# Scaling the tokens on ScalarE inside a mixture-of-experts unit, and adding the first product ahead of VectorE's other sums

## The chip, the cores and the metric

The kernel runs on one core of one Trainium2 chip. Its time is measured in microseconds on the device, as the median of several executions. One execution was also recorded by the hardware profiler; all rows below come from that one.

## The reference, cut to what matters

Attention with a sliding window gives 4608 tokens of 512 numbers. They go through eight experts, and every token's expert outputs are added with the weights of a Sinkhorn routing:

```python
for e in range(E):                       # E = 8
    h = np.maximum(x @ w1[e], 0.0)       # x: 4608 x 512, w1[e]: 512 x 1024
    ye = h @ w2[e]                       # w2[e]: 1024 x 512
    out += P[:, e:e + 1] * ye            # P: routing weights, 4608 x 8, none negative
```

Because no weight is negative, x may be multiplied by its weight before the first product: relu(P x w1) w2 = P relu(x w1) w2.

## The kernel before

The kernel has two parts. The first computes attention, gates and the Sinkhorn iterations, and with them experts 0 and 1 of all tokens, whose outputs it keeps in DRAM (`ysp`). The second part is the loop over `units` (N = 108). A unit is one expert `e` from 2 to 7 for one group `g` of 256 tokens (two blocks `m` of 128); the six experts of a group follow each other, and there are 18 groups. The order of all instructions is written out by hand: each engine executes its own in the order in which the code issues them, and waits only for data and for buffers.

A unit has two layers. The first layer of unit n is computed in step n of the loop, the second layer of unit n - 1 in the same step, woven between the first one's matmuls, so that TensorE always has something to do.

- **The first layer.** For experts 2 to 6, from step 6 on (85 units), it is a Strassen product with seven partial products (`part`, L968). They use three PSUM banks `pa`, `pb`, `pc` out of a pool of four (`pmm`), which are handed out in turn. ScalarE copies sums from bank to bank (L1114, L1118, L1123) and applies the relu (`relu`, L981); VectorE makes the slots 3 and 1 of `h` from PSUM and `s5` (L1128, L1132). The other units use four plain banks (`l1_bank`, L948, its relu on L957).
- **The second layer** (`product`, L1005) is seven Strassen products too, numbered 1 to 7. Each goes on summing into its half of a PSUM bank `psM` over the six experts of a group. Product 1 has a bank of its own, and is the last one issued in a step. `make_sums` (VectorE, L985 to L987) makes its operands from `h`.
- **The end of a group.** When the last expert of a group is through (`end`), `gather` (VectorE, L1047) adds products 3, 4, 5 and 2 out of PSUM into `acc` in the step after; in the step after that (`done`), it adds 6, 7 and 1, and `finish` stores `acc`. Matmuls of the next group have then begun to refill these banks: the product m of the new group's first expert overwrites the bank, and so waits for the `gather` of the old product m.
- **The tokens.** `load_x` brings a group's two blocks into `xtok`. `scale_x(n + 2)` multiplies them by the routing weights of the unit after next (L889; 128x512, half precision, the weight of a token being one number for each partition) into `xs`; `turn_xs(n + 2)` has two DMAs transpose them into `xset` (L901, issued by SP), and `sums_x` (VectorE, L913 to L915) makes the sums T1 to T4 that the Strassen parts read. When `scale_x` has scaled for expert 7, it loads the next group's tokens (L881).
- **The start of a group's sum.** `begin` (VectorE, L1020, L1023) sets `acc` to the weighted outputs of experts 0 and 1, one block in each of two steps. In the first group `xtok` lies in the memory of `acc`, so `begin` must come after the last `scale_x` of that group.

Before the loop, `scale_x(0)` and `scale_x(1)` are issued among the last matmuls of the first part (the "filler", whose relu is L127 and whose matmuls are L115 and L137).

VectorE's order in a step before the change: `make_sums`, in a `done` step products 6 and 7 into `acc`, `scale_x`, `begin` where due, L1128, L1132, in a `done` step product 1 into `acc`, `sums_x`.

Of the kernel before, what the change touches and what calls it, by code (L numbers as in the profile page):

```python
# [14 lines left out]
def kernel(  # L15
# [10 lines left out]
    nc = tc.nc  # L26
    AF = mybir.ActivationFunctionType
    ALU = mybir.AluOpType
# [50 lines left out]
    P_sb = L_sb  # L79
# [149 lines left out]
    if True:  # L229
# [459 lines left out]
        for n, (b, kb, u) in enumerate(steps):  # L689
# [94 lines left out]
            if 10 * b + at >= 66:  # L784
                i = 10 * b + at - 66
# [39 lines left out]
        for it in range(8):  # L825
# [4 lines left out]
                out=P_sb,  # L830
                in0=P_sb,
# [4 lines left out]
                out=cs_sb, in_=P_sb.rearrange("p c e -> p e c"), axis=AX.X, op=ALU.add  # L836
# [8 lines left out]
                out=P_sb,  # L845
                in0=P_sb,
                scalar=float(Ntok) / float(E),
                in1=ca_sb.unsqueeze(1).to_broadcast([P, NBLK, E]),
                op0=ALU.mult,
# [13 lines left out]
        units = [(g, e) for g in groups for e in range(2, E)]  # L863
# [9 lines left out]
        xtok = [acc.rearrange("p m d -> p (m d)").bitcast(FP16)[:, HD * i : HD * i + HD] for i in range(2)]  # L873
        xs = [xset[i // 2][:, 4 + 2 * (i % 2) : 6 + 2 * (i % 2), :].rearrange("p q n -> p (q n)") for i in range(4)]
# [4 lines left out]
        def load_x(g):  # L879
            for m in range(2):  # L880
                nc.sync.dma_start(out=xtok[m], in_=xd[2 * g + m])  # L881

        def scale_x(n):
            if n >= N:
                return
            g, e = units[n]
            for m in range(2):
                blk = 2 * g + m
                nc.vector.tensor_scalar(  # L889
                    out=xs[2 * (n % 2) + m], in0=xtok[m], scalar1=P_sb[:, blk, e : e + 1], scalar2=None, op0=ALU.mult  # L890
                )
            if e == E - 1 and n + 1 < N:
                if g == groups[0]:
                    xtok[:] = [per.tile([P, HD], FP16, name=f"xtok_{i}", tag="yo", bufs=YO) for i in range(2)]
                load_x(units[n + 1][0])
# [43 lines left out]
        def l1_bank(n, i):  # L939
            g, e = units[n]  # L940
            if i == 0:
                new_h(n)
            x = xset[n % 2][:, 0:4].rearrange("p q (d t) -> p (q d) t", t=P).rearrange("p (b d) t -> p d b t", b=2)
            ps = aps.tile([P, 2, HB], FP32, name=f"psh_{n}_{i}", tag="pmm", bufs=4)
            for f in range(2):
                ft = 2 * i + f
                for dt in range(NDT):
                    nc.tensor.matmul(  # L948
                        out=ps[:, f, :],
                        lhsT=W1L[e][:, dt, P * ft : P * ft + P],  # L950
                        rhs=x[:, dt],
                        start=(f == 0 and dt == 0),
                        stop=(dt == NDT - 1),
                        skip_group_check=True,
                    )
            fh, j = 2 * (i // 2), 2 * (i % 2)
            nc.scalar.activation(  # L957
                out=h[n][:, fh : fh + 2, j : j + 2, :].rearrange("p t f k -> p f t k"),
                in_=ps.rearrange("p f (t k) -> p f t k", t=2),
                func=AF.Relu,  # L960
            )
# [18 lines left out]
        def relu(n, slot, src):  # L980
            nc.scalar.activation(out=h[n][:, slot], in_=src, func=AF.Relu)  # L981
# [14 lines left out]
        def product(n, *which):  # L996
            if n < 0:
                return
            g, e = units[n]
            for m in which:  # L1000
                bk, half = BANK[m]
                if bk not in Ms:
                    Ms[bk] = mps.tile([P, 2, 2 * P], FP32, name=f"psM_{bk}")
                for f in range(NF2):
                    nc.tensor.matmul(  # L1005
                        out=Ms[bk][:, half, :],
                        lhsT=h[n][:, LEFT[m], f, :],
                        rhs=W2L[e][RIGHT[m]][:, f, :],
                        start=(e == 2 and f == 0 and half == 0),
                        stop=(ends(n) and f == NF2 - 1 and (half == 1 or m == 1)),  # L1010
                        skip_group_check=True,
                    )
# [5 lines left out]
        def begin(g, m):  # L1018
            blk = 2 * g + m
            nc.vector.tensor_scalar(  # L1020
                out=acc[:, m, :], in0=y[:, 0, m, :], scalar1=P_sb[:, blk, 0:1], scalar2=None, op0=ALU.mult
            )
            nc.vector.scalar_tensor_tensor(  # L1023
                out=acc[:, m, :], in0=y[:, 1, m, :], scalar=P_sb[:, blk, 1:2], in1=acc[:, m, :],
                op0=ALU.mult, op1=ALU.add,
            )

        def gather(g, *which):
            q4 = acc.rearrange("p m (c n) -> p (m c) n", c=2)
            for m in which:  # L1030
                bk, half = BANK[m]
                ps = Ms[bk][:, half, :]
                for lo, step, op in {
                    1: ((0, 3, ALU.add),),
                    2: ((2, 0, ALU.add), (3, 0, ALU.subtract)),
                    3: ((1, 2, ALU.add),),
                    4: ((0, 2, ALU.subtract),),
                    5: ((0, 0, ALU.subtract), (1, 0, ALU.add)),
                    6: ((3, 0, ALU.add),),
                    7: ((0, 0, ALU.subtract),),  # L1040
                }[m]:
                    if step:
                        a = q4[:, lo : lo + step + 1 : step, :]
                        p2 = ps.unsqueeze(1).to_broadcast([P, 2, HB])
                    else:
                        a, p2 = q4[:, lo, :], ps
                    nc.vector.tensor_tensor(out=a, in0=a, in1=p2, op=op)  # L1047
# [46 lines left out]
        for n in range(N):  # L1094
            g = units[n - 1][0]
            end = ends(n - 1)
            done, late = late, ()
            if n > 0:
                make_sums(n - 1)
            some((4, 1, 0, 3, 2)[n] if n < 5 else 0)  # L1100
            if 0 < n <= E - 3:
                quads_w1(units[n - 1][1])
            if done:
                gather(units[n - 2][0], 6, 7)
            scale_x(n + 2)
            if n > 0 and units[n - 1][1] in (4, 5):
                begin(g, units[n - 1][1] - 4)
            if strassen(n):
                new_h(n)
                s5 = s5s[:, n % 2]  # L1110
                pa = bank(n, "A")
                part(n, pa, "a11", B11, True)
                pb = bank(n, "B")
                nc.scalar.copy(out=pb, in_=pa)  # L1114
                product(n - 1, 3)
                pc = bank(n, "C")
                part(n, pc, "s1", T1, True)
                nc.scalar.copy(out=s5, in_=pc)  # L1118
                product(n - 1, 4)
                if end:  # L1120
                    gather(g, 3, 4)
                part(n, pb, "s2", T2)
                nc.scalar.copy(out=pc, in_=pb)  # L1123
                part(n, pa, "a12", B21)
                relu(n, 0, pa)
                product(n - 1, 5, 2)
                part(n, pb, "s3", T3)
                nc.vector.tensor_tensor(out=h[n][:, 3], in0=pb, in1=s5, op=ALU.add)  # L1128
                relu(n, 3, h[n][:, 3])
                part(n, pc, "s4", B22)  # L1130
                turn_xs(n + 2)
                nc.vector.tensor_tensor(out=h[n][:, 1], in0=pc, in1=s5, op=ALU.add)  # L1132
                relu(n, 1, h[n][:, 1])
                if done:
                    gather(units[n - 2][0], 1)
                sums_x(n + 1)
                if end:
                    gather(g, 5, 2)
                product(n - 1, 6, 7)
                part(n, pb, "a22", T4)  # L1140
                relu(n, 2, pb)
                product(n - 1, 1)
            else:
                if done:
                    gather(units[n - 2][0], 1)
                pairs = ((3, 4), (5, 2), (6, 7), (1,))
                for i in range(4):
                    l1_bank(n, i)
                    product(n - 1, *pairs[i])
                    if end and i in (0, 1):  # L1150
                        gather(g, *pairs[i])
                turn_xs(n + 2)
                sums_x(n + 1)
            if done:
                finish(units[n - 2][0])
            if n > 0 and units[n - 1][1] == 2:
                load_y(g)
            if end:
                late = (6, 7, 1)
            if n == N - E + 2:  # L1160
                load_w2(E - 1)
# [34 lines left out]
```

## Time and profile before

| | |
|---|---|
| three runs | 1035.68, 1036.04 and 1041.56 us; median 1036.04 |
| the profiled execution | 1037.82 us, of which the span of the records is 1034.8 us |
| TensorE matmuls busy | 1008.6 us, 97% of the span |
| VectorE busy | 765.8 us, 74% |
| ScalarE busy | 566.8 us, 55% |
| the scaling, L889 on VectorE | 216 instructions of 347 ns (204 of them from `xtok`: 62.1 us) |
| TensorE clock granted | 0.998 |

In the rows, PE is TensorE's matmuls, PEld its weight loads, DVE VectorE, ACT ScalarE, POOL GpSimd, SP the engine that issues most DMAs. A row of the timeline gives the start, the length, the engine, the line and operation, what is written and read, and in brackets how long the engine stood idle before and what ended that. A row of the waits gives who waited for whom: the sum, how often, and the longest. A row of the groups gives, after the bar, the busy time in us and the mean ns of one instruction.

### The profile page before, as it was taken

How to read it: one execution, taken by the hardware profiler on the slowest of the kernel's cores; microseconds unless marked ns; L12 is line 12 of the kernel's file. 1: busy time of each engine (PE TensorE's matmuls, PEld its weight loads, DVE VectorE, ACT ScalarE, POOL GpSimd, SP SyncE). 2: the span in 40 equal slices, each digit the busy share in tenths (PEclk: the TensorE clock that was granted, in tenths of full speed). 3: DMA queues.
4: the chain of work that ended last, by engine and by line, in shares of the span. 5: the costliest groups of instructions: out<-in, count | busy, mean ns of one | idle time of the engine just before them, and what ended most of it. 6: DMA issues, size and time to landing. Idle time of an engine off the chain costs nothing.

```text
span 1034.8 us, 26710 instructions
## 1 busy us (share of the span) xinstructions
PE 1008.6 (97%) x11079; PEld 803.6 (78%) x11079; DVE 765.8 (74%) x1720; ACT 566.8 (55%) x973; POOL 80.4 (8%) x143
## 2 busy tenths in 40 slices
PE   7999999999999999999999999999999999999998
PEld 5645444444544789999999999999999999999997
DVE  5735666656587698778777877877877877877876
ACT  6646554555333345555555555655655655655654
POOL 1313032315110000000000000000000000000000
PEclk9999999999999999999999999999999999999999
DMA  9997799889997323324423423424433432432461
GB/s 245 203 259 174 152 224 232 204 187 186 226 186 146 88 56 93 83 52 93 84 52 93 95 45 89 103 43 87 99 57 78 94 71 64 98 76 59 97 119 37
DMA packets 264427, 122.38 MB, mean 118 GB/s; under 512 B 201969, under 2 KB 255729, under 8 KB 264305
## 3 DMA queue, kind: packets, MB, share of 16 engines
q1 hardware_dynamic: 249568, 102.68, 43.4%
q0 software_dynamic: 14304, 17.84, 10.4%
q8 instruction: 86, 1.41, 0.6%
q14 instruction: 37, 0.29, 0.1%
q10 hardware_dynamic: 432, 0.16, 0.1%
HBM read 78.30 MB, written 23.59 MB: 98 GB/s over the span
## 4 chain that ended last, share of the span: by engine, by line
PE 66%; DVE 14%; issue 2%; DMA 0%; SPq 0%; ACT 0%; DVEq 0%
PE psM L1005 25%; PE psB L968 8%; PE psy L137 7%; PE psh L115 7%; PE psh L948 7%; PE psA L968 6%; PE psC L968 5%; DVE acc L1047 4%; DVE hs L1132 2%; DVE hs L986 1%; DVE hs L985 1%; DVE hs L1128 1%; DVE hs L987 1%; PE psN L468 1%; DVE xset L913 1%
## 5 line engine op out<-in xcount | busy, mean ns | idle before, releaser
L1005 PEld LDWEIGHTS <-hs 128*128 128x128 f16 x2996 | 275.8, 98 | 35.0 <-issue 10.0
L1005 PE MATMUL psM<-w2l,hs 128*128 128x256 f16 x1440 | 186.6, 273 | 0.4 <-DVE hs L985 0.4
L968 PEld LDWEIGHTS <-w1l 128*128 128x128 f16 x2720 | 173.3, 98 | 4.0
L981 ACT ACTIVATE hs<-hs 128x512 f16<-128x512 f16 x170 | 104.3, 630 | 124.5 <-DVE hs L1128 124.5
L115 PE MATMUL psh<-xT,w1t 128*128 128x512 f16 (+1 forms) x608 | 139.7, 368 | 2.8 <-DVE xT L517 2.4
L127 ACT ACTIVATE hT<-psh 128x512 f16<-128x512 f32 (+1 forms) x144 | 83.5, 586 | 103.8 <-PE psh L115 103.3
L1005 PE MATMUL psM<-more,hs 128*128 128x256 f16 x864 | 128.9, 272 | 8.0 <-DVE acc L1047 8.0
L137 PE MATMUL psy<-w2t,hT 128*128 128x512 f16 x576 | 134.3, 379 | 0.0
L985 DVE TENSOR_TENSOR hs<-hs 128x1024 f16<-128x1024 f16 x107 | 73.8, 690 | 80.4 <-ACT hs L957 53.6
L968 PEld LDWEIGHTS <-s 128*128 128x128 f16 x1632 | 108.3, 98 | 4.6
L957 ACT ACTIVATE hs<-psh 128x512 f16<-128x512 f32 x92 | 55.0, 597 | 98.9 <-PE psh L948 96.6
L968 PE MATMUL psA<-xset,w1l 128*128 128x128 f16 x1360 | 103.7, 219 | 0.0
L137 PEld LDWEIGHTS <-hT 128*128 128x128 f16 x576 | 53.5, 98 | 60.9 <-issue 1.5
L555 DVE CAST yo<-psy 128x512 f16<-128x512 f32 x68 | 46.9, 690 | 69.8 <-PE psy L137 61.8
L115 PEld LDWEIGHTS <-w1t 128*128 128x128 f16 x608 | 54.7, 98 | 54.2 <-issue 6.3
L1128 DVE TENSOR_TENSOR hs<-psB,s5s 128x512 f16<-128x512 f32 x85 | 58.7, 690 | 41.8 <-PE psB L968 41.7
L430 ACT ACTIVATE pt<-psS 128x1024 f16<-128x1024 f32 (+2 forms) x80 | 67.7, 851 | 31.7 <-PE psS L412 24.5
L968 PE MATMUL psB<-xset,s 128*128 128x128 f16 x1088 | 82.9, 219 | 0.0
L1047 DVE TENSOR_TENSOR acc<-acc,psM 128x256 f32<-128x256 f32 (+1 forms) x162 | 73.9, 502 | 1.1 <-PE psM L1005 1.1
L948 PE MATMUL psh<-xset,w1t 128*128 128x256 f16 x576 | 74.6, 273 | 0.0
L443 DVE TENSOR_TENSOR pt<-pt,mask 128x1024 f16<-128x1024 f16 (+2 forms) x80 | 50.4, 630 | 32.0 <-ACT pt L430 31.9
L986 DVE TENSOR_TENSOR hs<-hs 128x1024 f16<-128x1024 f16 x107 | 73.2, 684 | 0.0
(113 smaller groups left out, 1386.6 us busy)
## 6 DMA issues: line engine op xcount, KB each, us to landing
y<-ysp SPq DMA_DIRECT2D x36, 256.0 KB, 3.2
ysp<-yo SPq DMA_DIRECT2D x68, 128.0 KB, 3.1
v<-in_v_dram SPq DMA_DIRECT2D x32, 256.0 KB, 4.6
out_dram<-acc SPq DMA_DIRECT2D x31, 256.0 KB, 2.6
q<-in_q_dram SPq DMA_DIRECT2D x5, 1024.0 KB, 6.6
k<-in_k_dram SPq DMA_DIRECT2D x5, 1024.0 KB, 9.2
xtok<-xd SPq DMA_DIRECT2D x34, 128.0 KB, 2.1
w2t<-in_moe_w_dram POOLq DMA_DIRECT2D x4, 1024.0 KB, 10.5
```

The source lines that it names most:

```text
L115: nc.tensor.matmul(out=ps[:, 0:nt], lhsT=w1ts[e][:, dt, P * ft : P * ft + P], rhs=xT[:, at : at + nb, dt, :], start=(dt == 0), stop=(dt == ...
L127: nc.scalar.activation(out=st["hT"][:, ft, 0:nt], in_=ps[:, 0:nt], func=AF.Relu)
L137: nc.tensor.matmul(out=ps, lhsT=st["hT"][:, ft, P * ms : P * ms + P], rhs=w2ts[e][:, ft, :], start=(ft == 0), stop=(ft == NFT - 1),)
L430: nc.scalar.activation(out=pt[0:nk, :, 0 : nk + nn], in_=ps[0:nk, :, :, 0 : nk + nn].rearrange("p a y n -> p (a y) n"), func=AF.Exp, scale ...
L948: nc.tensor.matmul(out=ps[:, f, :], lhsT=W1L[e][:, dt, P * ft : P * ft + P], rhs=x[:, dt], start=(f == 0 and dt == 0), stop=(dt == NDT - 1 ...
L968: nc.tensor.matmul(out=ps[:, j, :], lhsT=SL[e][w][:, k, P * j : P * j + P], rhs=xset[n % 2][:, x, P * k : P * k + P], start=(start and j = ...
L981: nc.scalar.activation(out=h[n][:, slot], in_=src, func=AF.Relu)
L985: nc.vector.tensor_tensor(out=t[:, 4:6], in0=t[:, 0:2], in1=t[:, 2:4], op=ALU.add)
L986: nc.vector.tensor_tensor(out=t[:, 6:8], in0=t[:, 1:4:2], in1=t[:, 0:3:2], op=ALU.subtract)
L1005: nc.tensor.matmul(out=Ms[bk][:, half, :], lhsT=h[n][:, LEFT[m], f, :], rhs=W2L[e][RIGHT[m]][:, f, :], start=(e == 2 and f == 0 and half = ...
L1047: nc.vector.tensor_tensor(out=a, in0=a, in1=p2, op=op)
L1128: nc.vector.tensor_tensor(out=h[n][:, 3], in0=pb, in1=s5, op=ALU.add)
```

## The change

`scale_x` multiplies on ScalarE (`nc.scalar.mul`) instead of VectorE. Its call moves from the head of the step into it: in a Strassen step behind the relu of `pa`, in a plain step behind the second bank. The `gather` of product 1 moves from behind the sums out of PSUM (L1128, L1132) to directly behind that of products 6 and 7. `begin` comes one step later.

```diff
-                nc.vector.tensor_scalar(
-                    out=xs[2 * (n % 2) + m], in0=xtok[m], scalar1=P_sb[:, blk, e : e + 1], scalar2=None, op0=ALU.mult
-                )
+                nc.scalar.mul(out=xs[2 * (n % 2) + m], in_=xtok[m], mul=P_sb[:, blk, e : e + 1])
...
             if done:
                 gather(units[n - 2][0], 6, 7)
-            scale_x(n + 2)
-            if n > 0 and units[n - 1][1] in (4, 5):
-                begin(g, units[n - 1][1] - 4)
+                gather(units[n - 2][0], 1)
+            if n > 0 and units[n - 1][1] in (5, 6):
+                begin(g, units[n - 1][1] - 5)
             if strassen(n):
...
                 part(n, pa, "a12", B21)
                 relu(n, 0, pa)
+                scale_x(n + 2)
                 product(n - 1, 5, 2)
...
                 relu(n, 1, h[n][:, 1])
-                if done:
-                    gather(units[n - 2][0], 1)
                 sums_x(n + 1)
...
             else:
-                if done:
-                    gather(units[n - 2][0], 1)
                 pairs = ((3, 4), (5, 2), (6, 7), (1,))
                 for i in range(4):
                     l1_bank(n, i)
+                    if i == 1:
+                        scale_x(n + 2)
                     product(n - 1, *pairs[i])
```

## The prediction

> **What bounds the kernel now.** I read the page first, then the waits of TensorE, then the timeline of two units of the last stage.
>
> ```profile
> span 1034.8 us, 26710 instructions
> ...
> PE 66%; DVE 14%; issue 2%; DMA 0%; SPq 0%; ACT 0%; DVEq 0%
> ```
>
> ```profile
> PE psM L1005 <- DVE acc L1047: 8.0, 17, 0.6
> ...
> PE psM L1005 <- DVE hs L985: 0.4, 1, 0.4
> ```
>
> The chain that ended last is mostly TensorE, with 14% on VectorE. The waits say where VectorE gets into it: TensorE stood 17 times, 8.0 us in all, before a product into PSUM (L1005) until VectorE had added an older product into `acc` (L1047). There are 18 groups, and 17 of them are followed by another one, so this is one stall for each change of group. Ordinary units have none. An ordinary Strassen unit, from its first matmul (`psA`, 703.95) to that of the next (710.13) and that one's third bank (`psC`):
>
> ```profile
> 703.95 0.61 PE L968 MATMUL psA<-xset,w1l 128*128 128x128 f16 x8
> ...
> 706.42 0.57 ACT L1123 COPY psC<-psB 128x512 f32<-128x512 f32 x1 [0.35 <-PE psB L968]
> ...
> 706.90 0.60 ACT L981 ACTIVATE hs<-psA 128x512 f16<-128x512 f32 x1
> ...
> 708.20 0.69 DVE L1128 TENSOR_TENSOR hs<-psB,s5s 128x512 f16<-128x512 f32 x1 [0.25 <-PE psB L968]
> ...
> 708.92 1.23 ACT L981 ACTIVATE hs<-hs 128x512 f16<-128x512 f16 x2 [1.42 <-DVE hs L1128]
> ...
> 710.06 0.58 ACT L981 ACTIVATE hs<-psB 128x512 f16<-128x512 f32 x1
> ...
> 710.13 0.61 PE L968 MATMUL psA<-xset,w1l 128*128 128x128 f16 x8
> ...
> 711.01 0.61 PE L968 MATMUL psC<-xset,aux 128*128 128x128 f16 x8
> ```
>
> It takes 710.13 - 703.95 = 6.18 us. ScalarE idles 1.42 us in it, between the first relu (706.90) and the two that wait for VectorE's sums (708.92). Now the second unit of a group, the one in which `done` is set:
>
> ```profile
> 614.81 0.61 PE L968 MATMUL psA<-xset,w1l 128*128 128x128 f16 x8
> ...
> 617.76 0.60 ACT L981 ACTIVATE hs<-psA 128x512 f16<-128x512 f32 x1
> ...
> 618.72 0.61 DVE L889 TENSOR_SCALAR xs<-xtok,L_sb 128x512 f16<-128x512 f16 x2
> ...
> 619.24 0.68 DVE L1128 TENSOR_TENSOR hs<-psB,s5s 128x512 f16<-128x512 f32 x1
> ...
> 619.96 1.23 ACT L981 ACTIVATE hs<-hs 128x512 f16<-128x512 f16 x2 [1.60 <-DVE hs L1128]
> 620.11 0.61 PE L968 MATMUL psB<-xset,w1l 128*128 128x128 f16 x8
> 620.44 0.68 DVE L1047 TENSOR_TENSOR acc<-acc,psM 128x512 f32<-128x512 f32 x1
> ...
> 621.10 0.58 ACT L981 ACTIVATE hs<-psB 128x512 f16<-128x512 f32 x1
> 621.17 0.60 PE L1005 MATMUL psM<-more,hs 128*128 128x256 f16 x4 [0.45 <-DVE acc L1047]
> ...
> 621.61 0.61 PE L968 MATMUL psA<-xset,w1l 128*128 128x128 f16 x8
> ...
> 622.49 0.61 PE L968 MATMUL psC<-xset,s 128*128 128x128 f16 x8
> ```
>
> It takes 621.61 - 614.81 = 6.80 us, 0.62 more than an ordinary one. The product at 621.17 starts a new sum in the bank of product 1, and that bank is free only when the add of the old product 1 (620.44 to 621.12) has read it. That add stands last of VectorE's queue here, behind the two scalings (618.72) and the two sums out of PSUM (619.24 and the one after it). Nothing forces it there: the old product 1 was finished before this unit began.
>
> **The change, part by part.** (1) *The add of product 1 goes in front.* In the `done` unit it takes the place of the two scalings, which leave VectorE. It then runs at about 618.7 to 619.4, over 1 us ahead of 620.56, when TensorE could use the bank (620.11 plus the 0.45 that eight such matmuls take from start to start). The stall's full price is not the 0.45 shown, because a matmul's shown end comes later than the start of the next one: it is 621.17 - 620.56 = 0.61, which the 0.62 of the two unit lengths confirms. Over all 17: 8.0 us shown plus 17 x 0.16 for that overlap = 10.7 us. The stalls vary little, the longest being 0.6 as shown.
>
> What is late next: the sum out of `psB` (L1128). It stood behind two scalings and now stands behind one add:
>
> ```profile
> L981 ACT ACTIVATE hs<-hs 128x512 f16<-128x512 f16 x170 | 104.3, 630 | 124.5 <-DVE hs L1128 124.5
> ...
> L889 DVE TENSOR_SCALAR xs<-xtok,L_sb 128x512 f16<-128x512 f16 x204 | 62.1, 347 | 0.0
> ...
> L1047 DVE TENSOR_TENSOR acc<-acc,psM 128x512 f32<-128x512 f32 x54 | 35.2, 679 | 0.6 <-PE psM L1005 0.6
> ...
> L235 ACT ACTIVATE mask<-rel 128x256 f16<-128x256 f16 x8 | 2.8, 404 | 0.0
> ...
> L823 ACT ACTIVATE L_sb<-L_sb,mx_sb 128x288 f32<-128x288 f32 x1 | 0.5, 534 | 0.0
> ```
>
> The pair held VectorE 0.52 from start to the next start (618.72 to 619.24), the add about 0.60 (0.68 less the 0.08 by which neighbours overlap), so L1128 and the three relus behind it come 0.08 later: the last relu at 621.18, ending 621.76. The next unit's third bank is the one that this relu reads (four banks in turn, three for a unit). Its first matmul moves from 622.49 to 622.49 - 0.61 = 621.88. Slack 0.12, less some 0.04 for a semaphore. I take 0; bounds 0 and 17 x 0.3 = 5 us given back.
>
> (2) *The scaling on ScalarE*: 216 instructions, two for each of 108 units. The trace has no such instruction (half-precision source, a column of `P_sb` as the scale). Rows around it: the relu from SBUF, same size, 630 ns; the only activation with a per-partition operand (L823, 128x288) 534 ns, which scaled by 512/288 is at most 949; from below the 0.57 of the copy at 706.42. Between L235 and L823 lie 130 ns for 32 more columns and the operand, about 100 for the operand alone, so I take 630 + 100 = 730 ns, an estimate, and 0.64 from start to start, since activations that wait for nothing overlap 0.09 (706.42 + 0.57 against 706.90).
>
> In the ordinary unit the pair starts at about 707.41 and ends at 708.78; the next relu is released at 708.92. Nothing is later. Room there: 1.51 us until that relu slips, and 0.37 more until TensorE sees it, through the third bank of the next unit (the last relu ends 710.64, its bank is written at 711.01): 1.88 for the pair, 0.94 each. The 949 as a duration is 0.86 from start to start, so TensorE is not reached even at the upper bound. In the `done` unit the pair starts at 618.27, relu 3 is due at 620.04, slack 0.4.
>
> From the Trainium skill, "ScalarE: Activation LUTs", section "What ACT_TABLE_LOAD costs": an activation takes 186 ns + 0.833 per column and 93 for each per-partition operand. By that a scaling is 706 ns, an estimate from the page; the relu of the trace, 630, stands beside its 613; no run here has shown the operand yet, and the sum would be the same.
>
> In the units without Strassen (the last of each group and the first six) the pair goes between the relus of the second and the third bank:
>
> ```profile
> 606.64 0.60 ACT L957 ACTIVATE hs<-psh 128x512 f16<-128x512 f32 x1 [1.15 <-PE psh L948]
> ```
>
> A gap of 1.15 for a pair of 1.28: that relu comes some 0.1 late, the next gap takes it up; 0.
>
> (3) *What waits for the scaling.* It moves about 1.9 us back in the unit, and SP's queue with it: the loads of `xtok` (one unit of six) and the transposes stand behind it.
>
> ```profile
> 706.53 0.82 SPq L881 DMA_DIRECT2D xtok<-xd  x2
> ```
>
> ```profile
> L901 SPq DMA_TRANSPOSE xset<-xs x212: 1188/1192/2542, 345.4 to 1013.4; - x106
> ...
> DMA to landing us min/median/max: 2.4/2.5/5.7
> ```
>
> ```profile
> L881 SPq DMA_DIRECT2D xtok<-xd x34: 332/375/925, 362.1 to 973.5; - x34
> ...
> DMA to landing us min/median/max: 2.0/2.1/4.3
> ```
>
> Worst unit, with both: loads 708.8 to 709.6, transposes issued at 709.6 and 710.8, landed 713.3; their reader is the unit after next, from 703.95 + 2 x 6.18 = 716.3. The new `xtok` lands at 709.2 + 2.1 = 711.3 and is read by the next unit's pair at 713.6. If it were late, ScalarE's queue would hold three relus behind it. Price 0, with 2 to 3 us to spare.
>
> (4) *`begin` one unit later* (1.2 us of VectorE): it falls into units where VectorE idles before L1128 or has no Strassen sums: 0. In the first group it clears a wait:
>
> ```profile
> 374.60 1.04 PE L948 MATMUL psh<-xset,w1t 128*128 128x256 f16 x8
> ...
> 375.99 1.05 PE L1005 MATMUL psM<-w2l,hs 128*128 128x256 f16 x8 [0.35 <-DVE hs L985]
> ```
>
> Eight such matmuls go on after 0.87, here after 1.39: 0.5 us, a gain that I take; bounds 0 and 0.5.
>
> (5) *The four scalings ahead of the loop* now stand between relus of the last filler unit and wait for their loads:
>
> ```profile
> 325.36 0.90 SPq L881 DMA_DIRECT2D acc<-xd  x2
> ...
> 328.69 0.60 ACT L127 ACTIVATE hT<-psh 128x512 f16<-128x512 f32 x1 [1.99 <-PE psh L115]
> ...
> 331.08 3.62 PE L115 MATMUL psh<-xT,w1t 128*128 128x512 f16 x16
> ```
>
> ```profile
> acc<-xd SPq DMA_DIRECT2D x2, 128.0 KB, 3.2
> ```
>
> Loads land at 328.6 and 329.0, the four end at about 331.2, and the relu of 328.69 ends at 331.8 instead of 329.3. Its bank is wanted again by the second half of the run at 331.08, at 331.95. I take 0; up to 0.9 if a load lands 1.1 later, as one `xtok` did (4.3 beside the 3.2 here).
>
> **Sum.** 10.7 + 0.5 = 11.2 us off. The profiled execution took 1037.82 us (span 1034.8 and 3.0 around it), so 1026.6 by it. The median of the three runs is 1036.04, 1.8 below; on that basis 1024.8, or 1.08% less. One per cent, 10.4 us, is about what a measurement of this kernel can tell from no change, so the gain lies just beyond it.
>
> **The rivals.** *The wait is handed on.* With the add gone from the end, the third bank of the next unit is 0.08 away from being next. For it: that thin slack, on a chain (add, L1128, three relus) each link of which may be some hundredths longer. Against: ordinary units run the same chain without a wait. Given back 0.3 of each 0.62: 17 x 0.3 = 5.1, so 1030; all given back, about 1035.5.
>
> *ScalarE becomes the bound: slower.* Place: the relus behind the pair in all 85 Strassen units. Point: more than 0.94 us for each scaling from start to start. If one costs twice the relu from SBUF (1.26, or 1.17 start to start), each unit loses 2.34 - 1.88 = 0.46: 39 us against the 11 won, so 1064. Against: L823 shows no such factor. A rule speaks for it: the Trainium skill, "ScalarE: Activation LUTs", section "Rules for kernel authors", wants plain multiplications on VectorE, not ScalarE. The trace agrees on the single instruction (347 against 630 and more), but an instruction in ScalarE's 1.42 of idle time displaces nothing.
>
> *The change doesn't do what it says*: the stall has another cause, and the add's place is chance. Then 1036. Against it: the add ends at 621.12 and the product starts at 621.17.
>
> **How the numbers follow.** Forecast, all or nearly all of the stalls gone: 0.72 (1023.5 to 1027.5). Handed on in part, or another cause: 0.19 (1028 to 1036). Slower: 0.09. Predicted 1024.8. The range runs from 1022.5 (the same stalls a little dearer than shown) to 1031, the middle of the second case; about 0.15 lies outside. Faster by over 1% needs more than 10.4 of the 11.2, that is all of the small terms going as taken: 0.60. Within 1%: the rest of the forecast and most of the second case, 0.31. Slower by over 1%: 0.09.
>
> **What would show it.** Right: no wait of `psM` for `acc` among TensorE's waits; the `done` unit at 6.2 us; scalings of 0.65 to 0.75 us on ScalarE, and its wait for L1128 down from 1.42 to about 0.15; transposes about 1 us later with no wait of `psh` or of L913 for them. Wrong: a wait of `psC` for the relu of `psB`, or of `psA`, in the unit after a `done` unit; relus that start straight after a scaling in every unit; ScalarE waiting for `xtok`; or a `done` unit still at 6.8.

## The result, and the profile after

The changed kernel takes 1027.84 us (median of five runs, 1025.04 to 1028.74) against 1037.38 for the kernel before (1035.68 to 1041.56). The ratio of the means is 0.9898, with a 95% interval from 0.987 to 0.9927; that of the medians is 0.9908. So the change makes the kernel about 1% faster. The profiled execution took 1025.04 us, its span is 1023.2, that is 11.6 below the span of before. Lines behind the edits have moved up: L1005 of before is L1003, L1047 is L1045, L1128 is L1127, L981 is L979, L968 is L966; the scaling is still L889.

From the page after, the span and the chain that ended last, by engine:

```profile
span 1023.2 us, 26806 instructions
...
PE 82%; DMA 0%; issue 0%; DVE 0%; ACT 0%; ACTq 0%
```

VectorE's 14% of the chain are gone. TensorE's waits after, the longest ones:

```profile
PE psN L468 <- DVE pt L443: 3.9, 8, 1.0
PE psh L115 <- DVE xT L517: 2.6, 2, 1.5
PE psT L351 <- ACT c L289: 2.4, 3, 1.3
PE psh L946 <- DMA xset<-xset: 1.6, 1, 1.6
```

All but the last are of the first part of the kernel. The 17 waits of `psM` for `acc` (8.0 us) are gone, and so is the one for `make_sums`. The groups after, the scaling on its new engine, the relus behind it, and the wide adds into `acc`:

```profile
L889 ACT ACTIVATE xs<-xtok,L_sb 128x512 f16<-128x512 f16 x204 | 135.6, 719 | 0.0
...
L979 ACT ACTIVATE hs<-hs 128x512 f16<-128x512 f16 x170 | 104.3, 630 | 24.3 <-DVE hs L1127 24.3
...
L1045 DVE TENSOR_TENSOR acc<-acc,psM 128x512 f32<-128x512 f32 x54 | 35.4, 683 | 2.0
```

A scaling takes 719 ns on ScalarE, and its idle time ahead of the two relus of each unit fell from 124.5 us to 24.3. The timeline of an ordinary unit after:

```profile
696.60 0.61 PE L966 MATMUL psA<-xset,w1l 128*128 128x128 f16 x8
...
699.55 0.60 ACT L979 ACTIVATE hs<-psA 128x512 f16<-128x512 f32 x1
700.04 1.33 ACT L889 ACTIVATE xs<-xtok,L_sb 128x512 f16<-128x512 f16 x2
...
701.58 1.23 ACT L979 ACTIVATE hs<-hs 128x512 f16<-128x512 f16 x2 [0.21 <-DVE hs L1127]
...
702.79 0.61 PE L966 MATMUL psA<-xset,w1l 128*128 128x128 f16 x8
```

It is as long as before, 702.79 - 696.60 = 6.19 us. And a `done` unit after:

```profile
608.91 0.61 PE L966 MATMUL psA<-xset,w1l 128*128 128x128 f16 x8
...
611.10 0.69 DVE L984 TENSOR_TENSOR hs<-hs 128x1024 f16<-128x1024 f16 x1
...
611.82 0.43 DVE L985 TENSOR_TENSOR hs<-hs 128x512 f16<-128x512 f16 x1
...
612.16 1.54 DVE L1045 TENSOR_TENSOR acc<-acc,psM 128x256 f32<-128x256 f32 x3
612.35 1.33 ACT L889 ACTIVATE xs<-xtok,L_sb 128x512 f16<-128x512 f16 x2
...
613.34 1.04 PE L1003 MATMUL psM<-w2l,hs 128*128 128x256 f16 x8
613.61 0.68 DVE L1127 TENSOR_TENSOR hs<-psB,s5s 128x512 f16<-128x512 f32 x1
...
614.35 0.61 PE L966 MATMUL psB<-xset,w1l 128*128 128x128 f16 x8
614.79 0.60 PE L1003 MATMUL psM<-more,hs 128*128 128x256 f16 x4
615.23 0.61 PE L966 MATMUL psA<-xset,w1l 128*128 128x128 f16 x8
```

It takes 615.23 - 608.91 = 6.32 us, down from 6.80, but not 6.18. The product into its own bank (614.79) now follows the matmuls into `psB` without a wait. Those matmuls (614.35) are late instead: they should follow the product at 613.34 after 0.87, at 614.21. They accumulate into the bank that the sum at 613.61 reads until 614.29. This wait of 0.14 stands in no list of waits, because the shown end of these matmuls lies 0.16 behind the start of the ones that follow without a wait. The Trainium skill, "Perfetto Trace Analysis", section "Tensor Engine Instruction (MATMUL, LD_WEIGHTS)", says that these ends are estimated and not observed; the trace agrees, with those 0.16 us.

Where the 11.6 us of the two spans came from is read from three places. First the same step of the Sinkhorn iterations, ahead of everything that the change touches, before and then after:

```profile
318.72 0.28 PE L841 MATMUL psC<-cs_sb,ones 128*128 128x8 f32 x2
```

```profile
316.43 0.28 PE L841 MATMUL psC<-cs_sb,ones 128*128 128x8 f32 x2
```

2.3 us of the difference are there already, by chance: the first matmul of the loop came between 339.15 and 343.17 us in the profiled executions of before, of the changed kernel and of e1 to e4 below. Then that first matmul and the first Strassen unit, before and after:

```profile
341.44 3.66 PE L948 MATMUL psh<-xset,w1l 128*128 128x256 f16 x32
...
379.93 0.61 PE L968 MATMUL psA<-xset,w1l 128*128 128x128 f16 x8
```

```profile
339.15 3.66 PE L946 MATMUL psh<-xset,w1l 128*128 128x256 f16 x32
...
377.13 0.61 PE L966 MATMUL psA<-xset,w1l 128*128 128x128 f16 x8
```

38.49 us became 37.98: 0.5. From there to the end of the span, 654.87 became 646.07: 8.8, of which the 17 `done` units are 17 x 0.48 = 8.2; two of them, at 7.02 and 6.97 us before, give another 0.4. So the change is worth 9.3 us by the traces, 9.5 by the medians and 10.5 by the means.

### The profile page after: what moved, and what is told of

It is laid out like the page before. It is cut to its first block, busy times and chain, and to the rows that moved or that the text cites. A ratio compares the mean times of both kernels' runs of the same rounds, so it can differ in the third digit from the quotient of the medians.

```text
span 1023.2 us, 26806 instructions
## 1 busy us (share of the span) xinstructions
PE 1006.3 (98%) x11079; PEld 801.8 (78%) x11079; DVE 713.4 (70%) x1504; ACT 694.5 (68%) x1189; POOL 78.0 (8%) x143
## 3 DMA queue, kind: packets, MB, share of 16 engines
q0 software_dynamic: 14304, 17.84, 10.5%
## 4 chain that ended last, share of the span: by engine, by line
PE 82%; DMA 0%; issue 0%; DVE 0%; ACT 0%; ACTq 0%
PE psM L1003 32%; PE psB L966 11%; PE psh L946 8%; PE psA L966 7%; PE psC L966 7%; PE psy L137 7%; PE psh L115 7%; PE psN L468 1%; PE psS L412 1%; PE psy L1064 0%; DMA xset<-xset 0%; PE psG L527 0%; PE psX L506 0%; PE psC L841 0%; DVE acc L1072 0%
## 5 line engine op out<-in xcount | busy, mean ns | idle before, releaser
L1003 PEld LDWEIGHTS <-hs 128*128 128x128 f16 x2996 | 275.3, 98 | 24.3
L1003 PE MATMUL psM<-w2l,hs 128*128 128x256 f16 x1440 | 186.6, 273 | 0.0
L966 PEld LDWEIGHTS <-w1l 128*128 128x128 f16 x2720 | 173.2, 98 | 6.2 <-issue 0.5
L889 ACT ACTIVATE xs<-xtok,L_sb 128x512 f16<-128x512 f16 x204 | 135.6, 719 | 0.0
L1003 PE MATMUL psM<-more,hs 128*128 128x256 f16 x864 | 129.0, 273 | 0.0
L983 DVE TENSOR_TENSOR hs<-hs 128x1024 f16<-128x1024 f16 x107 | 73.9, 691 | 73.6 <-ACT hs L955 43.4
L1127 DVE TENSOR_TENSOR hs<-psB,s5s 128x512 f16<-128x512 f32 x85 | 58.6, 690 | 89.9 <-ACT xs L889 74.3
L979 ACT ACTIVATE hs<-hs 128x512 f16<-128x512 f16 x170 | 104.3, 630 | 24.3 <-DVE hs L1127 24.3
L966 PEld LDWEIGHTS <-s 128*128 128x128 f16 x1632 | 108.3, 98 | 4.6
L966 PE MATMUL psA<-xset,w1l 128*128 128x128 f16 x1360 | 103.7, 219 | 0.0
L966 PE MATMUL psB<-xset,s 128*128 128x128 f16 x1088 | 82.9, 219 | 0.0
L1045 DVE TENSOR_TENSOR acc<-acc,psM 128x256 f32<-128x256 f32 (+1 forms) x162 | 74.1, 504 | 2.2
```

What stands on the lines that cost most here:

```text
L889: nc.scalar.mul(out=xs[2 * (n % 2) + m], in_=xtok[m], mul=P_sb[:, blk, e : e + 1])
L966: nc.tensor.matmul(out=ps[:, j, :], lhsT=SL[e][w][:, k, P * j : P * j + P], rhs=xset[n % 2][:, x, P * k : P * k + P], start=(start and j = ...
L983: nc.vector.tensor_tensor(out=t[:, 4:6], in0=t[:, 0:2], in1=t[:, 2:4], op=ALU.add)
L1003: nc.tensor.matmul(out=Ms[bk][:, half, :], lhsT=h[n][:, LEFT[m], f, :], rhs=W2L[e][RIGHT[m]][:, f, :], start=(e == 2 and f == 0 and half = ...
```

## The experiments

Three questions were asked: are both parts of the change needed (e1, e2), what are the 0.14 us that are left in each `done` unit (e3, e4, e8), and how much room does ScalarE have, and where (e5 to e7)? My theory for the second: the add of product 1 reads quarters of `acc` that the adds of 6 and 7 write, so it cannot overlap with the one ahead of it, and the sum behind it comes too late for `psB`. The rival: ScalarE's longer queue.

Each ratio below is to the kernel before, run beside the experiment: 1036.21 us for e1 to e4, 1038.44 for e5 to e8. The changed kernel was not run beside them, so a time told against its 1027.84 is good to a microsecond or two only.

**e1, the add alone.** The kernel before with this:

```diff
             if done:
                 gather(units[n - 2][0], 6, 7)
+                gather(units[n - 2][0], 1)
             scale_x(n + 2)
...
                 relu(n, 1, h[n][:, 1])
-                if done:
-                    gather(units[n - 2][0], 1)
...
             else:
-                if done:
-                    gather(units[n - 2][0], 1)
```

> The kernel before, with one part of the change: the add of product 1 stands directly behind those of 6 and 7, the scalings stay on VectorE behind it. Theory (VectorE's queue in the done unit decides, and both parts are needed): the sum out of psB (L1128 of before) now waits behind one add more, ends at about +5.9 us of the unit, and the next matmuls into psB (a22, due at +5.3) wait some 0.6 us for it. The done unit stays at 6.7 to 6.9 us, the time within 2 us of before. Rival (the add's place alone is the gain, the move to ScalarE only makes room nowhere needed): done unit 6.2 to 6.35, some 8 us faster than before.

Measured: 1037.81 us, ratio 1.0016 (1.0004 to 1.0028): nothing won. TensorE's waits in it:

```profile
PE psB L968 <- DVE hs L1129: 9.1, 17, 0.8
```

The 17 waits are still there, before `psB` instead of `psM`, and a `done` unit takes 6.84 us, as expected. Moving the add without making room for it exchanges one wait for another.

**e2, the scaling alone.** The changed kernel with the add of product 1 back behind the two sums:

```diff
                 gather(units[n - 2][0], 6, 7)
-                gather(units[n - 2][0], 1)
...
                 relu(n, 1, h[n][:, 1])
+                if done:
+                    gather(units[n - 2][0], 1)
```

> The other part alone: scalings on ScalarE inside the unit, begin one step later, the add of product 1 at its old place behind both sums out of PSUM. Theory: those sums start some 0.25 us earlier, the add ends about 0.3 us after the product wants its bank; done unit 6.5 to 6.55 us, ordinary unit 6.18, time about 5 us below before (1032). Rival (ScalarE's longer queue costs something in every unit): ordinary units above 6.2, time not below before.

Measured: 1032.75 us, ratio 0.9958 (0.9943 to 0.9974), within a microsecond of what was expected. The old wait is shorter, but there, in the sum and in a `done` unit:

```profile
PE psM L1003 <- DVE acc L1045: 4.7, 17, 0.3
```

```profile
614.76 0.61 PE L966 MATMUL psA<-xset,w1l 128*128 128x128 f16 x8
...
620.94 0.60 PE L1003 MATMUL psM<-more,hs 128*128 128x256 f16 x4 [0.28 <-DVE acc L1045]
...
621.38 0.61 PE L966 MATMUL psA<-xset,w1l 128*128 128x128 f16 x8
```

The unit takes 6.62 us, a little over the 6.50 to 6.55 expected.

So the scaling's move brings 3.5 us (1036.21, the kernel before on that chip, to 1032.75), the add's move nothing by itself, and both together over 9. The rival of e2, a time not below before, is out.

**e3, the gap filled.** In `done` steps the third sum of `make_sums`, 128x512, goes between the adds:

```diff
         def make_sums(n):
...
-            nc.vector.tensor_tensor(out=t[:, 1], in0=t[:, 0], in1=t[:, 3], op=ALU.add)
...
+            def last_sum():
+                if n > 0:
+                    t = h[n - 1]
+                    nc.vector.tensor_tensor(out=t[:, 1], in0=t[:, 0], in1=t[:, 3], op=ALU.add)
+
             if n > 0:
                 make_sums(n - 1)
+            if not done:
+                last_sum()
...
                 gather(units[n - 2][0], 6, 7)
+                last_sum()
                 gather(units[n - 2][0], 1)
```

> The changed kernel, with the third sum of make_sums (128x512, h slot 1, read only by product 1 at the end of the step) moved in done steps from ahead of the adds of 6 and 7 to between them and the add of product 1. Theory (the 0.14 us left in each done unit is a22 waiting for the sum out of psB, which is late because the add of 1 must wait for the add of 7 to have written acc, some 0.1 to 0.2 us idle on VectorE): that idle time is filled, the sum starts 0.15 to 0.2 earlier, done unit 6.18 to 6.22, time 2 to 2.4 us below the changed kernel. Rival (the rest comes from ScalarE, whose relus are later): done unit stays at 6.32.

Measured: 1026.26 us, ratio 0.9892 (0.9875 to 0.991). By time this can't be told from the changed kernel; the units tell it. The `done` unit of e3:

```profile
611.59 0.61 PE L966 MATMUL psA<-xset,w1l 128*128 128x128 f16 x8
...
614.38 0.75 DVE L1044 TENSOR_TENSOR acc<-acc,psM 128x256 f32<-128x256 f32 x2
...
615.04 0.42 DVE L1098 TENSOR_TENSOR hs<-hs 128x512 f16<-128x512 f16 x1
...
615.38 0.68 DVE L1044 TENSOR_TENSOR acc<-acc,psM 128x512 f32<-128x512 f32 x1
...
615.98 0.69 DVE L1134 TENSOR_TENSOR hs<-psB,s5s 128x512 f16<-128x512 f32 x1
...
617.78 0.61 PE L966 MATMUL psA<-xset,w1l 128*128 128x128 f16 x8
```

617.78 - 611.59 = 6.19: the rest is gone, although ScalarE's work is the same, and the rival falls. The sum out of `psB` starts 4.39 into the unit instead of 4.70 in the changed kernel, and each of VectorE's rows here starts before the one ahead has ended. These 0.31 us are more than the 0.15 to 0.2 expected, because the edit closes two gaps. About 0.20 is the gap between the adds. The other 0.11 lay ahead of the third sum: it writes slot 1 of `h`, which the sum ahead of it reads, and in the changed kernel it starts 0.72 after that one (611.10 to 611.82), where sums that touch different data start 0.61 apart. Without the gap between the adds alone, the sum would by these figures have ended at 614.09 in the changed kernel, ahead of the 614.21 at which `psB` is due; that is an estimate, since e3 closes both gaps at once.

**e4, shorter scalings.** `mul=1.0` instead of `mul=P_sb[:, blk, e : e + 1]`; the routing weights of experts 2 to 7 are left out.

> The changed kernel, with the scalings by the constant 1.0 instead of the column of routing weights: the weights of experts 2 to 7 are left out of the result. Theory (0.09 us of a scaling is its per-partition operand, and ScalarE has room in every unit): scalings of 630 ns instead of 720, done unit still 6.32, time that of the changed kernel within 1 us. Rival (the rest of 0.14 us in a done unit comes from the longer scalings): done unit 6.2 or less and some 2 us faster.

Measured: 1026.71 us, ratio 0.9905 (0.9889 to 0.9921). The scaling, and a `done` unit:

```profile
L889 ACT ACTIVATE xs<-xtok 128x512 f16<-128x512 f16 x204 | 117.0, 629 | 0.0
```

```profile
609.38 0.61 PE L966 MATMUL psA<-xset,w1l 128*128 128x128 f16 x8
...
615.69 0.61 PE L966 MATMUL psA<-xset,w1l 128*128 128x128 f16 x8
```

629 ns, so the operand is worth 90, and the unit stays at 6.31. A pair of scalings that is 0.18 us shorter takes nothing off the rest.

**e5 and e6, more scalings.** The changed kernel with one and with two scalings repeated in each unit, e5 with `if m == 1:` ahead of the added line:

```diff
                 nc.scalar.mul(out=xs[2 * (n % 2) + m], in_=xtok[m], mul=P_sb[:, blk, e : e + 1])
+                nc.scalar.mul(out=xs[2 * (n % 2) + m], in_=xtok[m], mul=P_sb[:, blk, e : e + 1])
```

> The changed kernel with every second block scaled twice (the same result written again), so three scalings a unit on ScalarE. Theory of the prediction (up to 1.88 us of scalings fit between the first relu and the point from which TensorE waits): three take about 1.83 from start to start, so the relus behind them come some 0.3 us later and nothing waits; ordinary units 6.18, time that of the changed kernel within 1 us. Rival (ScalarE has no room beyond the 0.2 us that it still idles there): 0.4 us in each of 85 units, some 34 us slower than the changed kernel.

> The changed kernel with both blocks scaled twice, four scalings a unit. Theory: they take about 2.44 us, 0.5 to 0.56 more than the 1.88 there are, which TensorE waits out ahead of psC in the next unit, for the relu of psB; ordinary units 6.7, 43 to 48 us slower than the changed kernel (1071 to 1076). Rival (other slack takes it up): less than 10 us.

Three cost nothing in an ordinary unit, which stays at 6.18 us: 1028.26 us, ratio 0.9899 (0.9868 to 0.9929). Four cost 32 us against the changed kernel, fewer than the 43 to 48 expected: 1060.05, ratio 1.0198 (1.0151 to 1.0245). TensorE's longest wait with four, and a unit:

```profile
PE psB L967 <- ACT psB L1113: 15.4, 66, 0.5
```

```profile
708.24 0.61 PE L967 MATMUL psA<-xset,w1l 128*128 128x128 f16 x8
...
709.12 0.61 PE L967 MATMUL psC<-xset,s 128*128 128x128 f16 x8
709.29 0.57 ACT L980 ACTIVATE hs<-psB 128x512 f16<-128x512 f32 x1
...
709.76 0.58 ACT L1113 COPY psB<-psA 128x512 f32<-128x512 f32 x1
...
710.40 0.61 PE L967 MATMUL psB<-xset,s 128*128 128x128 f16 x8 [0.23 <-ACT psB L1113]
```

That the waiting begins between three and four is as expected, the place is not. The matmuls into `psC` start at 709.12, before the relu of the last unit's `psB` has even begun (709.29): they are in another bank. What waits are the matmuls into the new `psB` (due at 708.24 + 1.77 = 710.01, started at 710.40) for the copy of `psA`, which stands behind that relu in ScalarE's queue. Four scalings start over 4 x 0.61 = 2.44 us, and 0.39 of it is waited for, so 2.05 us fit. TensorE waits so in 66 of the 85 units. The first Strassen unit of each group, 17 in all, still takes 6.18, and one near the end takes 9.99, the cause of which stays open. The expectation had all 85 units pay, and 0.5 to 0.56 each.

**e7, at the head of the step.** The scalings on ScalarE, in Strassen steps at VectorE's old place:

```diff
             if strassen(n):
+                scale_x(n + 2)
                 new_h(n)
...
                 relu(n, 0, pa)
-                scale_x(n + 2)
```

> The changed kernel with the scalings still on ScalarE, but in Strassen steps at the head of the step, where VectorE had them, ahead of the copy of psA to psB. Theory (ScalarE has room only between the first relu and the next two): the copy is done about 2.3 us into the unit, 0.55 us after the matmuls that add to it want to start (1.77); ordinary units 6.7 to 6.8, some 45 to 55 us slower than the changed kernel. Rival (ScalarE idles over 2 us in each unit, so any place serves): no slower.

Measured: 1064.48 us, ratio 1.0246 (1.0217 to 1.0276), 37 slower than the changed kernel.

```profile
711.86 0.61 PE L966 MATMUL psA<-xset,w1l 128*128 128x128 f16 x8
...
712.26 1.32 ACT L889 ACTIVATE xs<-xtok,L_sb 128x512 f16<-128x512 f16 x2
...
713.49 0.59 ACT L1113 COPY psB<-psA 128x512 f32<-128x512 f32 x1
...
714.12 0.61 PE L966 MATMUL psB<-xset,s 128*128 128x128 f16 x8 [0.33 <-ACT psB L1113]
```

The matmuls due at 713.63 start at 714.12, 0.49 late. The mechanism is the expected one. The loss is below the 45 to 55, in part because the copy ended 2.2 us into the unit and not 2.3, and in part because the first Strassen unit of each group pays less: it takes 6.53 us. 68 x 0.49 + 17 x 0.35 = 39.3, less the 17 x 0.14 that the changed kernel loses itself, is 36.9, beside the 37 measured. Where the scaling stands in ScalarE's queue decides whether it costs anything.

**e8, the add between the sums.** The changed kernel with the add of product 1 behind the first sum out of PSUM:

```diff
                 gather(units[n - 2][0], 6, 7)
-                gather(units[n - 2][0], 1)
...
                 relu(n, 3, h[n][:, 3])
+                if done:
+                    gather(units[n - 2][0], 1)
                 part(n, pc, "s4", B22)
```

> The changed kernel with the add of product 1 between the two sums out of PSUM (L1127 and L1131 of the changed kernel) instead of ahead of both. Theory: a22 no longer waits for the first sum, but the second sum and with it the relus come 0.5 us later, and psC of the next unit waits 0.1 to 0.2 us for the relu of psB: the unit after a done unit gets that time, done and next unit together are again 12.5 us or a little above, time as the changed kernel within 2 us. Rival (a22's wait was all there is): both units at 6.18, 2.3 us faster than the changed kernel.

Here the rival was right, and the expected wait of `psC` did not come. Measured: 1025.15 us, ratio 0.9871 (0.9842 to 0.99), and the `done` unit:

```profile
610.13 0.61 PE L966 MATMUL psA<-xset,w1l 128*128 128x128 f16 x8
...
615.43 0.61 PE L966 MATMUL psB<-xset,w1l 128*128 128x128 f16 x8
...
616.31 0.61 PE L966 MATMUL psA<-xset,w1l 128*128 128x128 f16 x8
...
616.84 0.58 ACT L979 ACTIVATE hs<-psB 128x512 f16<-128x512 f32 x1
...
617.20 0.61 PE L966 MATMUL psC<-xset,s 128*128 128x128 f16 x8
```

It takes 6.18 us, as the unit after it does, and the matmuls into `psC` start at 617.20 in the middle of the relu that they were expected to wait for. As in e6, that dependence does not exist. e3 and e8 both beat the two kernels unit by unit, by 17 x 0.14 = 2.4 us against the changed one; by time, their intervals overlap with its own.

## Why the prediction was right, and where not

- *The stall and its cause*: right. The 17 waits are gone, and e1 and e2 show that it takes both parts. That the add's old place was chance (the third rival) is out by e2: its wait shrank as the add came earlier.
- *The size of the main term*: 10.7 us were forecast, 8.8 measured from the first Strassen unit on. The step that failed is "what is late next". It let the sum out of `psB` start 0.08 later and put the next wait at `psC`. The sum starts 4.70 into the unit, where it was 4.43 (619.24 - 614.81), so 0.27 later, and the wait is at `psB`, 0.14 for each group. Two things were missed. First, the add of 1 doesn't overlap with the add of 7, whose result it reads: its idle time is 2.0 us in the group row above, 0.12 for each of 17, and the usual overlap of 0.08 is lost as well. These 0.20 and the 0.08 that were forecast give 0.28, beside the 0.27 measured. Before, the scalings lay between. The row's idle time is 2.0 in e4 to e7 too, where the two adds are neighbours, and 0.2 in e2, e3 and e8, where they are not. That it is the data that the add waits for is read from the code, and no run changes the data alone. Second, the matmuls of the seventh part (a22) write the bank that the sum reads; that slack was thin before, too, 620.11 against the sum's end at 619.92.
- *The rival "handed on"* named the right kind of loss, about a quarter of the stall given back, but the wrong bank. Its premise, four banks given out in turn, which the description of the kernel states too, is refuted by e6 and e8: the third bank of a unit is not the one that the last relu of the unit before reads.
- *The scaling*: 730 ns estimated, 719 measured, start to start 0.61 for 0.64. Nothing in an ordinary unit became longer. Both terms of that estimate were right: 630 and 629, and 90 for the operand where 100 was taken. The Trainium skill, "ScalarE: Activation LUTs", section "What ACT_TABLE_LOAD costs", gives 93 for the operand; the 90 agree.
- *ScalarE's room*: 1.88 forecast, 2.05 by e6, with three scalings free in e5. That the two lie close is luck: 1.88 ends at a wait of `psC` for the relu of `psB`, which does not exist, and the 2.05 end at the copy of `psA` behind that relu. The slower rival stayed away for the reason given: the rule that spoke for it in the prediction holds for the single instruction (719 against 347 ns), not for the time.
- *Transposes and loads*: TensorE waits for none of them, beyond the one of 1.6 us (`psh` for `xset`) that was there already. But the forecast had no wait of VectorE's sums of x for the transposes either, and there are three (L911 for `xset`, 0.9 us in all); no unit became longer by them.
- *`begin` and the first group*: 0.5 us forecast, 0.5 measured. It comes with the scaling and `begin`, since the 38.49 us stay 38.49 in e1 and are 37.98 in e2; which of the two it is, no run separates. *The four scalings ahead of the loop*: 0 forecast, 0 measured; the first matmul of the loop follows the step of 318.72 or 316.43 after 22.7 us in both. The room there was nearly used up: with six scalings (e5) and eight (e6) it is 23.9 and 24.5.
- *The sum*: 11.2 forecast, 9.3 by the traces and 9.5 by the medians. "Just beyond" 1% was forecast, and that is not shown: the interval, 0.7 to 1.3%, does not tell on which side of 1% the gain lies.

## What to carry to other kernels

When an instruction is moved out of a queue, ask what was hidden behind it: here the removed scalings had also covered the time between two adds of which one reads the other's result. An instruction may move to an engine that is slower for it, if it lands in idle time of which both the start and the next customer are known; the same move 3 us earlier in the unit cost 37 us. Gains of a few microseconds are better read from the length of repeating units, which agree to 0.01 us, than from whole executions that differ by more before the change even begins.

## What the hardware showed that was not expected

On VectorE, neighbours that touch different data overlap by 0.08 us in these traces, while the add of product 1, which reads what the add ahead of it wrote, starts 0.12 after that one's end: 1.54 us for three adds instead of about 1.34. This is no price for every such pair: of the sums of x in the same unit, L912 reads what L911 wrote and starts 0.03 after its end (614.81 + 0.42, then 615.26). Why the adds wait longer stays open.

The Trainium skill, "VectorE: DVE Perf Modes", section "The DRAIN you can't avoid", has a semaphore between two VectorE instructions cost nothing extra. Here the pair of adds cost 0.2 more than an independent one, and one instruction in between (e3) took that time for its own work; whether a semaphore is what costs here, no run shows.
